# A spectral mixer with a token MLP, forward and backward, on one core: an opening put in another order, and more buffers for the last output

## Chip, cores, metric

The kernel runs on one core of one Trainium2 chip. The metric is device time in microseconds (us) of that core; lower is better. A profile is one execution with the hardware profiler on. Its span runs from the first to the last instruction and is about 2 us shorter than the time of the same run (367.6 us of 369.41 us for the kernel before).

## The reference

The reference is one layer with its gradients. `A_x` is 2048 tokens (S) by 448 features (D); F is 1792. All arrays are bfloat16.

```python
def _A_ref(x, w_r, w_i):                     # spectral mixer
    X = rfft2(x.astype(float32), axes=(-2, -1))
    X = X * (w_r + 1j * w_i)                 # (2048, 225)
    return irfft2(X, s=(S, D), axes=(-2, -1)).astype(bfloat16)

def _B_ref(x, w1, b1, w2, b2):               # MLP over the tokens
    h = layernorm(x)
    u = gelu(einsum("bsd,sf->bdf", h, w1) + b1)
    y = einsum("bdf,fs->bds", u, w2) + b2
    return y.transpose(0, 2, 1)

h   = x + _A_ref(layernorm(x), w_r, w_i)
out = h + _B_ref(layernorm(h), w1, b1, w2, b2)
# returned: out, then the gradients of x, w_r, w_i, w1, b1, w2, b2 for a given grad_out
```

## The kernel before

The Fourier transforms are matmuls. Their sine and cosine matrices are made on the core: GpSimd makes index patterns (iota), VectorE and GpSimd do the integer work, ScalarE takes the sine. The first transform goes tile by tile, 16 tiles of 128 tokens, each scaled by its LayerNorm factor (`rstd`).

In the gaps of the transform TensorE does "fill" work that doesn't depend on it: the matmuls of `w2` with `grad_out`, which the backward pass needs. For them `w2` must come in transposed, in 14 pieces of 128 x 2048 (512 KB each). A DMA transposes each piece on its way, into a ring of five buffers. All loads, transposes and stores are issued in program order by one engine, SyncE, so they form one queue. Its first part:

```python
    w2T_ring = Ring(ring(rE, 0, 3, NT, P).views + ring(rO, S, 2, NT, P).views)   # 5 buffers

    def load_w2T():
        j = w2T_ring.i
        if j == NFB:                         # NFB = 14
            return
        wT = w2T_ring.next()
        nc.sync.dma_start_transpose(out=wT, in_=B_w2[j * P:(j + 1) * P, :].rearrange("f (t c) -> f t c", c=P))
        w2Ts.append(wT)

    def load_x(q):                           # a quarter: 4 tiles of x, 448 KB
        nc.sync.dma_start(out=xn[:, 4 * q:4 * q + 4, :], in_=x_pt[:, 4 * q:4 * q + 4, :])

    load_x(0)
    load_go(0)                               # a quarter of grad_out
    load_w2T()
    load_go(1)
    load_x(1)
    load_go(2)
    load_go(3)
    load_w2T()
    load_x(2)
    load_w2T()
    load_x(3)
```

The fill lets the next transpose go when it is done with one; from the ninth on (`CAP = 8`) it holds them back until the second stage of the transform:

```python
    def dg_gen():
        for j in range(NFB):
            wT = w2Ts.pop(0)
            ...                              # 16 matmuls, one eviction
                    if w2T_ring.i >= cap[0]: # cap = [CAP]
                        held_w2.append(load_w2T)
                    else:
                        load_w2T()
...
    def fwd_x(c2):                           # at the start of the second stage
        if c2 == 0:
            for kind in "TWWWWTTT":          # T: a held transpose, W: a load of the imaginary weights w_i
                if kind == "W":
                    next(w_loads)
                elif held_w2:
                    held_w2.pop(0)()
```

The opening, and the point where the LayerNorm factors of tiles 4 and 5 come from GpSimd:

```python
    pcol = col()
    iota(pcol, [[0, 1]], 1)
    ...                                      # two more iotas
    r_ops = []
    gen_R(Later(ve, r_ops), Later(sc, r_ops))          # two 128x64 tensor_scalar first, then a Sin
    ...
    sc.activation(out=warm, in_=eps_x, func=ACT.Sqrt)  # fetches the square-root table
    zero_pads()                                        # four GpSimd memsets
    ...
    iota(base[:, :, :, 0], [[1, 16], [128, 16]])       # two 128x256 iotas
    ...
    for t in range(2):
        ln_stats(xn, t, mvx)
    ...
    Rs = {t: scale_R(t) for t in range(2)}
    for t in range(2, 4):
        ln_stats(xn, t, mvx)
    ...
    uv = gen_UV()                            # GpSimd: decode, masks
    ...
    for t in (4, 5):
        ln_stats(xn, t, mvx)
    newton_gp(mvx[:, 4:6, 1], rstd_x[:, 4:6], slice(4, 6))   # 1/sqrt on GpSimd
    fill(6)
```

The last work is the gradient of a weight, `gw_gen`. It evicts into a ring of six buffers (`ost`), and one store sends each buffer to memory:

```python
    ost = ring(rO, 0, 6, S // 2)

    def gw_gen(n, rhs, width, store):
        ...
                os_ = [ost.next(), ost.next()]
        ...
            def out(pw, w, c, i):
                evac(out=o[:, x:x + w], in_=pw[i][:, 0:w])
                if x:
                    defer(1.5, lambda j=2 * u + i: store(j, 512 * (c - 1), x + w, o), o)
```

Of the kernel before, what the change touches and what calls it, by code (L numbers as in the profile page):

```python
# [13 lines left out]
ALU = mybir.AluOpType  # L14
ACT = mybir.ActivationFunctionType
AX = mybir.AxisListType

P = 128
S = 2048
D = 448  # L20
# [99 lines left out]
def kernel(  # L120
# [20 lines left out]
    nc = tc.nc  # L141
# [4 lines left out]
    gp_ = nc.gpsimd  # L146
# [28 lines left out]
    def ps_mm():  # L175
        return psum.tile([P, 512], F32, tag="mm", bufs=4, name="ps_mm")
# [75 lines left out]
    def col(n=1):  # L252
        i = _ci[0]
        _ci[0] += n
        assert _ci[0] <= 64
        return cols[:, i:i + n]
# [32 lines left out]
    def load_w2T():  # L289
        j = w2T_ring.i  # L290
        if j == NFB:
# [4 lines that stand above are left out]
# [4 lines left out]
    def load_x(q):  # L300
        nc.sync.dma_start(out=xn[:, 4 * q:4 * q + 4, :], in_=x_pt[:, 4 * q:4 * q + 4, :])
# [1 line left out]
    def load_go(q):  # L303
        nc.sync.dma_start(out=go_tp[:, 4 * q:4 * q + 4, :], in_=go_tp_d[:, 4 * q:4 * q + 4, :])

    load_x(0)
    load_go(0)
    load_w2T()
    load_go(1)
    load_x(1)  # L310
    load_go(2)
# [13 lines left out]
    def ftmp(off, *dims):  # L325
        n = int(np.prod(dims))
        v = tf[:, off:off + n]
        if len(dims) == 1:
            return v
        names = "abcd"[:len(dims)]  # L330
        return v.rearrange("p (" + " ".join(names) + ") -> p " + " ".join(names),
                           **{c: d for c, d in zip(names, dims)})

    def iota(ap, pattern, ch=0):
        gp_.iota(ap, pattern=pattern, base=0, channel_multiplier=ch, allow_small_or_imprecise_dtypes=True)

    def floor_div(eng, out, in_, n):
        eng.tensor_scalar(out=out, in0=in_, scalar1=float(np.float32(1.0 / n)),
                          scalar2=float(-0.5 + 0.5 / n), op0=ALU.mult, op1=ALU.add)
        eng.tensor_scalar(out=out, in0=out, scalar1=MAGIC, scalar2=MAGIC, op0=ALU.add, op1=ALU.subtract)  # L340

    pcol = col()
    iota(pcol, [[0, 1]], 1)
# [49 lines left out]
    def gp_madd(out, in0, scalar, in1):  # L393
        gp_.tensor_scalar(out=gtmp, in0=in0, scalar1=scalar, scalar2=None, op0=ALU.mult)  # L394
        gp_.tensor_tensor(out=out, in0=gtmp, in1=in1, op=ALU.add)  # L395
# [33 lines left out]

    def decode(eng):  # L430
        a4, fc, s_, c_, f_ = col(), col(), col(), col(), col()
        floor_div(eng, a4, pcol, 64)
        gp_madd(s_, a4, -64.0, pcol)
        floor_div(eng, fc, s_, 8)
        gp_madd(s_, fc, -8.0, s_)
        gp_madd(s_, s_, 2.0, a4)
        floor_div(eng, c_, fc, 4)
        gp_madd(f_, c_, -4.0, fc)
        return fc, s_, c_, f_
# [77 lines left out]
    def gen_inv_cols(ch):  # L517
        e, en = col(), col()
        inv_cols[ch] = (e, en)
        gp_.memset(e, 2.0)  # L520
        if ch == 0:
            gp_.memset(e[0:1, :], 1.0)
        else:
            gp_.tensor_scalar(out=e, in0=pcol, scalar1=112.0, scalar2=None, op0=ALU.is_equal)
            gp_.tensor_scalar(out=e, in0=e, scalar1=-1.0, scalar2=2.0, op0=ALU.mult, op1=ALU.add)
            gp_.memset(e[0:1, :], 0.0)
        gp_.tensor_scalar(out=en, in0=e, scalar1=-1.0, scalar2=None, op0=ALU.mult)
        gp_.tensor_scalar(out=halves[:, ch:ch + 1], in0=e, scalar1=-0.5, scalar2=1.5, op0=ALU.mult, op1=ALU.add)
# [86 lines left out]

    def zero_pads():
        for f in fold_ring.views:
            gp_.memset(f[:, 896:912], 0.0)

    def fold_prep(src, t2):  # L620
        ft = fold_ring.next()
# [177 lines left out]
    def rstd_of(a, b):  # L799
        return newton(mvx[:, a:b, 1], rstd_x[:, a:b], slice(a, b))  # L800

    r_ops = []
    gen_R(Later(ve, r_ops), Later(sc, r_ops))
    warm = col()
    fwd_ops = gen_fwd_d()
    for fn in r_ops:
        fn()
    for fn in fwd_ops[:4]:
        fn()
    sc.activation(out=warm, in_=eps_x, func=ACT.Sqrt)  # L810
    zero_pads()
    base = ftmp(3072, 16, 16, 2)
    fix = ftmp(3584, 16)
    iota(base[:, :, :, 0], [[1, 16], [128, 16]])
    gp_.iota(base[:, :, :, 1], pattern=[[1, 16], [-128, 16]], base=1920, channel_multiplier=0,
             allow_small_or_imprecise_dtypes=True)
# [24 lines left out]
    fold_prep(xn, 1)  # L841
    for t in (4, 5):
        ln_stats(xn, t, mvx)
    newton_gp(mvx[:, 4:6, 1], rstd_x[:, 4:6], slice(4, 6))
    fill(6)
    turn_biases = load_biases()
    Meter.side, Meter.every, Meter.count = [], 1, 0
# [352 lines left out]
    ost = ring(rO, 0, 6, S // 2)  # L1200
    o4 = out_4.rearrange("(p t) f -> p t f", t=NT)

    def gw_gen(n, rhs, width, store):
        for u in range(n // 2):
            st = ahead.pop(0)

            def whole(pw, w, c, i, k, start, stop):
                mm(pw[i][:, 0:w], lhsT=st[:, 4 * i + k, :], rhs=rhs(c, k, 0, P), start=start, stop=stop)

            def parts(pw, w, c, start):  # L1210
                for i in range(2):
                    mm(pw[i][:, 0:w], lhsT=st[64 * i:64 * i + 64, 3, :], rhs=rhs(c, 3, 64 * i, 64 * i + 64),
                       start=start, stop=not start)

            def out(pw, w, c, i):
                o = os_[i]
                x = c % 2 * 512
                evac(out=o[:, x:x + w], in_=pw[i][:, 0:w])
                if x:
                    if c == 3 and i:  # L1220
                        st_load()
                    defer(1.5, lambda j=2 * u + i: store(j, 512 * (c - 1), x + w, o), o)

            for c in range(0, 4, 2):
                os_ = [ost.next(), ost.next()]
                pw = [ps_mm(), ps_mm()]
                for i in range(2):
                    for k in range(3):
                        whole(pw, 512, c, i, k, k == 0, False)
                        yield  # L1230
                w = min(512, width - 512 * (c + 1))
                pv = [ps_mm(), ps_mm()]
                parts(pw, 512, c, False)
                parts(pv, w, c + 1, True)
                for i in range(2):
                    out(pw, 512, c, i)
                yield
                yield
                for i in range(2):
                    for k in range(3):  # L1240
                        whole(pv, w, c + 1, i, k, False, k == 2)
                        if k == 2:
                            out(pv, w, c + 1, i)
                        yield

    pending.append(gw_gen(NFB, lambda c, k, a, b: goT[a:b, k, c * 512:(c + 1) * 512], S,
                          lambda j, a, n, o: nc.sync.dma_start(out=out_6[j * P:(j + 1) * P, a:a + n], in_=o[:, 0:n])))
    pending.append(gw_gen(NT, lambda c, k, a, b: du_t[a:b, 4 * c:min(NFB, 4 * c + 4), k, :], F,
                          lambda t, a, n, o: nc.sync.dma_start(out=o4[:, t, a:a + n], in_=o[:, 0:n])))
    nc.sync.dma_start(out=rC[:, 0:NG * 2 * KW], in_=w_d[:])  # L1250
    for t in range(NT - LAG, NT + 2):
        if t == NT - 2:
# [78 lines left out]
```

## Time and profile before

| | before |
|---|---|
| time, median of 3 runs | 370.2 us (369.69 to 370.56) |
| profiled span, mean granted clock | 367.6 us, 0.991 |
| TensorE busy | 346.1 us, 94% |
| TensorE idle, start of the span to the first matmul | 8.0 us |
| last matmul to the end of the span | 6.3 us |

In these lines PE is TensorE, PEld its weight loads, DVE VectorE, ACT ScalarE, POOL GpSimd, SP SyncE. The first fence is from the page of the kernel before: the span, each engine's busy time with its share and number of instructions, TensorE's busy tenths in 40 equal slices of the span, and the chain of waits by engine.

```profile
span 367.6 us, 6387 instructions
...
PE 346.1 (94%) x2114; PEld 185.8 (51%) x2121; DVE 255.8 (70%) x641; ACT 203.7 (55%) x426; POOL 73.7 (20%) x240
...
PE   1888999899999999999999999999999999999993
...
PE 77%; DVE 6%; POOL 5%; DMA 4%; ACT 4%; issue 2%; POOLq 0%; DVEq 0%; ACTq 0%
```

TensorE is nearly full except in the first and last slices, and it is most of the chain. The next fence is the table of stretches of the kernel before: from and to, length, then busy time (and instructions) of PE, PEld, DVE, ACT and POOL, the granted TensorE clock, the DMA engines' mean busy share (packets overlap, so it can pass 1), and GB/s.

```profile
0.00:14.00 14.00, 5.74 (x26) 2.95 (x27) 10.98 (x36) 7.32 (x14) 11.84 (x65) 1.00 0.92 253
14.00:30.00 16.00, 13.17 (x88) 7.82 (x86) 12.56 (x45) 8.67 (x18) 11.24 (x49) 0.89 1.14 220
30.00:46.00 16.00, 15.33 (x131) 10.89 (x132) 13.04 (x39) 12.49 (x25) 5.07 (x21) 1.00 1.06 199
46.00:62.00 16.00, 15.74 (x112) 9.62 (x110) 9.42 (x25) 9.20 (x20) 0.22 (x2) 1.00 1.03 194
```

TensorE leaves little time free after 30 us. (A share near 1 says that the engines are busy, not how many bytes they move: it goes with 194 to 253 GB/s here, and with 371 GB/s from 361 to 364 us.) From the timeline of the opening of the kernel before (start, duration, engine, line, operation, output and input; in brackets the idle time before it and what ended it):

```profile
1.25 0.49 POOL L335 IOTA r<- 128x448 f32 x1
1.32 2.08 DVE L79 TENSOR_SCALAR r<-r,cols 128x64 int32<-128x64 f32 x2
...
1.65 4.34 SPq L294 DMA_TRANSPOSE rE<-in_B_w_dram  x1
...
4.05 1.28 ACT L79 ACT_TABLE_LOAD   x1 [4.05 <-DVE r L79]
...
7.99 0.58 PE L215 MATMUL ps_ff<-rX,rS 128*128 128x128 bf16 x4 [7.99 <-DVE rX L79]
...
15.62 0.55 PE L215 MATMUL ps_mm<-rC,rE 128*128 128x448 bf16 x2 [0.54 <-DMA rE<-in_B_w_dram]
...
19.25 0.25 DVE L79 TENSOR_SCALAR rX<-Rm,rstd_x 128x128 bf16<-128x128 bf16 x1 [3.40 <-POOL rstd_x L376]
```

The 128x64 pair on VectorE takes 2.08 us, beside GpSimd's iotas. The sine table comes at 4.05 us, the first matmul at 7.99. At 15.62 TensorE waits for the second transpose of `w2`. At 19.25 VectorE has waited 3.40 us for GpSimd's `rstd`: that is the scaling of tile 4, which the rest of the opening follows.

From the same kernel, the queue of SyncE (how long the issue of each group held it) and TensorE around the tenth transpose:

```profile
41.54 5.96 SPq L655 DMA_DIRECT2D r<-r  x3
47.59 2.24 SPq L294 DMA_TRANSPOSE rO<-in_B_w_dram  x1
49.89 2.34 SPq L571 DMA_DIRECT2D rB<-in_A_w_i_dram  x4
52.34 4.30 SPq L294 DMA_TRANSPOSE rO<-in_B_w_dram  x1
...
59.52 0.55 PE L215 MATMUL ps_mm<-rC,rO 128*128 128x448 bf16 x2 [0.26 <-DMA rO<-in_B_w_dram]
```

`r<-r` are the reshapes of the first transform's result for the second stage. The tenth transpose is issued at 52.34 us and TensorE takes it up at 59.52. It waited only 0.26 us. And the end of the kernel before, where the last buffers wait for stores:

```profile
358.25 3.08 PE L215 MATMUL ps_mm<-r,rS 128*128 128x512 bf16 x18
...
360.83 0.86 ACT L79 CAST rO<-ps_mm 128x512 bf16<-128x512 f32 x2 [1.36 <-DMA out_dram<-rO]
362.17 1.02 DVE L79 CAST rO<-ps_mm 128x512 bf16<-128x512 f32 x2 [3.24 <-DMA out_dram<-rO]
...
363.82 0.81 SPq L1249 DMA_DIRECT2D out_dram<-rO  x2
```

### The profile page before, as it was taken

Reading aid. Unit: us, or ns where it says so; the run is one execution under the profiler, and the core shown is the slowest. Engines: PE = TensorE matmul, PEld = TensorE weight load, DVE = VectorE, ACT = ScalarE, POOL = GpSimd, SP = SyncE. Lnnn points to the kernel's source line nnn. Section 1 sums busy time; section 2 is a strip of 40 time slices with the busy share of each in tenths; the row PEclk is TensorE's granted clock in tenths of the full one; section 3 lists DMA queues with packets and bytes.
Section 4 is the critical chain, followed back from the end, with each engine's and each line's share of the span. In section 5 each row is a group of like instructions: output and inputs, shape, how many; then the busy total and the mean of one; then the engine's idle time right before and its main releaser. Section 6 shows DMA issues by size and latency. Waiting matters only on the chain.

```text
span 367.6 us, 6387 instructions
## 1 busy us (share of the span) xinstructions
PE 346.1 (94%) x2114; PEld 185.8 (51%) x2121; DVE 255.8 (70%) x641; ACT 203.7 (55%) x426; POOL 73.7 (20%) x240
## 2 busy tenths in 40 slices
PE   1888999899999999999999999999999999999993
PEld 0455766455645555555555566653444444555541
DVE  7698839973876888583247766674787883788881
ACT  3738748756966454413312454463576664576751
POOL 8867000000220000010002221100000000465650
PEclk9989999999999999999999999999999999999998
DMA  8999989648999999998868789379669899798997
GB/s 205 308 219 215 168 202 183 146 130 288 294 293 351 326 305 244 190 289 183 189 154 167 157 188 171 75 227 312 208 204 231 242 199 261 241 201 273 203 211 231
DMA packets 148249, 81.63 MB, mean 222 GB/s; under 512 B 95544, under 2 KB 140600, under 8 KB 147832
## 3 DMA queue, kind: packets, MB, share of 16 engines
q1 hardware_dynamic: 148216, 81.23, 90.3%
q8 instruction: 16, 0.26, 0.3%
q14 instruction: 17, 0.14, 0.1%
HBM read 27.56 MB, written 23.89 MB: 140 GB/s over the span
## 4 chain that ended last, share of the span: by engine, by line
PE 77%; DVE 6%; POOL 5%; DMA 4%; ACT 4%; issue 2%; POOLq 0%; DVEq 0%; ACTq 0%
PE ps_mm L215 62%; PE ps_ff L215 15%; DMA out_dram<-rO 2%; DMA rO<-in_B_w_dram 2%; DVE rS L79 2%; ACT rO L79 2%; DVE r L79 1%; ACT Ut L79 1%; DVE stats L79 1%; DVE rO L79 1%; DVE rA L79 1%; POOL cols L394 1%; POOL cols L395 1%; DVE rX L79 1%; ACT rAT L79 0%
## 5 line engine op out<-in xcount | busy, mean ns | idle before, releaser
L215 PEld LDWEIGHTS <-r 128*128 128x128 bf16 (+1 forms) x628 | 60.3, 105 | 49.2 <-issue 1.8
L215 PEld LDWEIGHTS <-rS 128*128 128x128 bf16 (+2 forms) x528 | 44.8, 99 | 48.6 <-issue 10.1
L79 ACT CAST rO<-ps_mm 128x512 bf16<-128x512 f32 (+1 forms) x75 | 40.3, 567 | 25.0 <-PE ps_mm L215 21.6
L1130 POOL TENSOR_SCALAR lcol<-lcol 128x1 f32<-128x1 f32 x32 | 18.6, 580 | 148.0 <-ACT r L79 148.0
L215 PE MATMUL ps_mm<-rD,r 128*128 128x448 bf16 x224 | 44.5, 352 | 0.0
L79 DVE CAST rO<-ps_mm 128x512 bf16<-128x512 f32 (+1 forms) x45 | 28.4, 644 | 19.3 <-PE ps_mm L215 16.0
L215 PEld LDWEIGHTS <-rst 128*128 128x128 bf16 (+1 forms) x320 | 24.0, 97 | 29.0 <-issue 13.1
L215 PE MATMUL ps_mm<-rC,rE 128*128 128x448 bf16 x144 | 37.1, 377 | 0.8 <-DMA rE<-in_B_w_dram 0.5
L79 ACT CAST r<-ps_ff 128x452 bf16<-128x452 f32 x54 | 28.9, 537 | 11.0 <-PE ps_ff L215 10.6
L215 PE MATMUL ps_mm<-rG,rst 128*128 128x512 bf16 (+1 forms) x155 | 34.0, 380 | 0.2
L215 PE MATMUL ps_mm<-rB,r 128*128 128x448 bf16 x160 | 31.1, 352 | 0.1
L215 PE MATMUL ps_mm<-r,rst 128*128 128x512 bf16 (+3 forms) x160 | 31.2, 353 | 0.0
L79 ACT ACTIVATE r<-ps_mm,rstd_h 128x448 bf16<-128x448 f32 x16 | 10.1, 634 | 29.3 <-PE ps_mm L215 29.3
L215 PE MATMUL ps_ff<-csI,rAT 113*128 113x448 bf16 x108 | 24.9, 353 | 0.4 <-ACT rAT L79 0.2
L79 DVE SCALAR_TENSOR_TENSOR r<-ps_mm,b2col,r 128x448 bf16<-128x448 f32 x16 | 10.9, 682 | 19.9 <-PE ps_mm L215 18.4
L79 ACT ACTIVATE r<-rC 128x448 bf16<-128x448 bf16 x16 | 9.1, 571 | 26.8 <-DMA out_dram<-r 21.8
L79 ACT ACTIVATE rG<-rG 128x896 bf16<-128x896 bf16 x14 | 13.3, 950 | 14.9 <-DVE rG L79 14.7
L215 PE MATMUL ps_mm<-rE,rS 128*128 128x448 bf16 x112 | 21.5, 352 | 0.0
L215 PEld LDWEIGHTS <-rO 128*128 128x128 bf16 (+1 forms) x165 | 15.6, 98 | 10.9 <-DMA rO<-in_B_w_dram 0.6
L79 ACT CAST rS<-ps_ff 128x512 bf16<-128x512 f32 x30 | 17.7, 589 | 5.1 <-PE ps_ff L215 5.1
L215 PEld LDWEIGHTS <-rE 128*128 128x128 bf16 x148 | 14.6, 103 | 9.6 <-issue 2.8
L215 PE MATMUL ps_mm<-rC,rO 128*128 128x448 bf16 x80 | 19.1, 352 | 0.3 <-DMA rO<-in_B_w_dram 0.3
(173 smaller groups left out, 604.3 us busy)
## 6 DMA issues: line engine op xcount, KB each, us to landing
out_dram<-rO SPq DMA_DIRECT2D x44, 256.0 KB
r<-in_B_w_dram SPq DMA_DIRECT2D x5, 1024.0 KB
r<-r SPq DMA_DIRECT2D x16, 226.0 KB
r<-r SPq DMA_DIRECT2D x32, 113.0 KB
rS<-in_B_w_dram SPq DMA_DIRECT2D x4, 896.0 KB
out_dram<-r SPq DMA_DIRECT2D x32, 112.0 KB
out_dram<-rO SPq DMA_DIRECT2D x16, 192.0 KB
rO<-in_B_w_dram SPq DMA_DIRECT2D x2, 1024.0 KB
```

Source lines behind the costliest of these rows:

```text
L79: fn(**kw)
L215: nc.tensor.matmul(out, lhsT=lhsT, rhs=rhs, start=start, stop=stop)
L394: gp_.tensor_scalar(out=gtmp, in0=in0, scalar1=scalar, scalar2=None, op0=ALU.mult)
L395: gp_.tensor_tensor(out=out, in0=gtmp, in1=in1, op=ALU.add)
L1130: gp_.tensor_scalar(out=m1, in0=ms, scalar1=-1.0 / D, scalar2=None, op0=ALU.mult)
```

## The change

The change wants TensorE to start earlier and to stop later work from waiting.

- ScalarE loads the sine table at once, by a dummy sine.
- Half a quarter of x comes first, then the first transpose, then grad_out and the other half.
- GpSimd's big iotas wait for a VectorE copy (`pcolb`) and a memset, so that they don't run beside VectorE's first operations; the pad memsets go to VectorE.
- Twelve idle matmuls on zeros are to raise TensorE's clock.
- The `rstd` of tiles 4 and 5 moves from GpSimd to VectorE.
- The last output gets 14 buffers in place of 6: eight in a region (`rG`) that is free by then.

```diff
-    load_x(0)
+    nc.sync.dma_start(out=xn[:, 0:2, :], in_=x_pt[:, 0:2, :])
+    load_w2T()
     load_go(0)
-    load_w2T()
+    nc.sync.dma_start(out=xn[:, 2:4, :], in_=x_pt[:, 2:4, :])
     load_go(1)
@@
+    warm = col()
+    nc.vector.memset(warm, 0.0)
+    sc.activation(out=warm, in_=warm, func=ACT.Sin)
+    nc.vector.memset(rAT[:, 0:512], 0.0)
+    idle = ps_mm()
+    for _ in range(12):
+        nc.tensor.matmul(idle[:, 0:D], lhsT=rAT[:, 0:P], rhs=rAT[:, 0:D], start=True, stop=True)
@@ decode, and one more place
-        floor_div(eng, a4, pcol, 64)
-        gp_madd(s_, a4, -64.0, pcol)
+        floor_div(eng, a4, pcolb, 64)
+        gp_madd(s_, a4, -64.0, pcolb)
@@ zero_pads, now called before gen_R
-            gp_.memset(f[:, 896:912], 0.0)
+            nc.vector.memset(f[:, 896:912], 0.0)
@@
+    pcolb = col()
+    ve.tensor_copy(out=pcolb, in_=pcol)
+    nc.vector.memset(base[:, 0, 0:1, 0], 0.0)
+    nc.vector.memset(base[:, 0, 0:1, 1], 0.0)
     iota(base[:, :, :, 0], [[1, 16], [128, 16]])
@@
-    newton_gp(mvx[:, 4:6, 1], rstd_x[:, 4:6], slice(4, 6))
+    for fn in rstd_of(4, 6):
+        fn()
@@
-    def gw_gen(n, rhs, width, store):
+    def gw_gen(n, rhs, width, store, ost):
@@ the first call passes ost, the second
+                          Ring(ring(rG, 0, 8, S // 2).views + ost.views)))
```

More of the change, by code (lines that the diff above doesn't have):

```diff
@@ L523, in gen_inv_cols @@
         else:
-            gp_.tensor_scalar(out=e, in0=pcol, scalar1=112.0, scalar2=None, op0=ALU.is_equal)
+            gp_.tensor_scalar(out=e, in0=pcolb, scalar1=112.0, scalar2=None, op0=ALU.is_equal)
             gp_.tensor_scalar(out=e, in0=e, scalar1=-1.0, scalar2=2.0, op0=ALU.mult, op1=ALU.add)
@@ L800, in rstd_of @@
         return newton(mvx[:, a:b, 1], rstd_x[:, a:b], slice(a, b))
+    zero_pads()
     r_ops = []
     gen_R(Later(ve, r_ops), Later(sc, r_ops))
-    warm = col()
     fwd_ops = gen_fwd_d()
@@ L810 @@
     sc.activation(out=warm, in_=eps_x, func=ACT.Sqrt)
-    zero_pads()
     base = ftmp(3072, 16, 16, 2)
     fix = ftmp(3584, 16)
+    pcolb = col()
+    ve.tensor_copy(out=pcolb, in_=pcol)
+    nc.vector.memset(base[:, 0, 0:1, 0], 0.0)
+    nc.vector.memset(base[:, 0, 0:1, 1], 0.0)
     iota(base[:, :, :, 0], [[1, 16], [128, 16]])
@@ L1246 @@
     pending.append(gw_gen(NFB, lambda c, k, a, b: goT[a:b, k, c * 512:(c + 1) * 512], S,
-                          lambda j, a, n, o: nc.sync.dma_start(out=out_6[j * P:(j + 1) * P, a:a + n], in_=o[:, 0:n])))
+                          lambda j, a, n, o: nc.sync.dma_start(out=out_6[j * P:(j + 1) * P, a:a + n], in_=o[:, 0:n]), ost))
     pending.append(gw_gen(NT, lambda c, k, a, b: du_t[a:b, 4 * c:min(NFB, 4 * c + 4), k, :], F,
-                          lambda t, a, n, o: nc.sync.dma_start(out=o4[:, t, a:a + n], in_=o[:, 0:n])))
+                          lambda t, a, n, o: nc.sync.dma_start(out=o4[:, t, a:a + n], in_=o[:, 0:n]),
+                          Ring(ring(rG, 0, 8, S // 2).views + ost.views)))
     nc.sync.dma_start(out=rC[:, 0:NG * 2 * KW], in_=w_d[:])
```

## The prediction

> **What bounds the kernel now.** TensorE: the page gives it 346.1 us busy of a 367.6 us span; the chain of waits is matmuls for 77%. Its idle time sits mostly at the ends (timeline, stretches): 8.0 us before the first matmul, 2.4 us between 14 and 20 us, 6.2 us after the last matmul ends at 361.3. Its clock is 0.5 from 20 to 23.7 us.
>
> **The opening before.** The chain up to 19.25 us is almost all GpSimd.
> 1. VectorE's two 128x64 tensor_scalar start at 1.32 us and last 2.08 us together, ending when GpSimd's run of iotas and memsets ends (3.31 us). The Trainium skill (SBUF — State Buffer, "SBUF: two separate sides") says that VectorE in a two-port mode and GpSimd lock each other out for a whole instruction. The times agree; the cause isn't shown.
> 2. ScalarE loads the sine table only at 4.05 us (1.28 us), the square-root table at 5.76; the first matmul starts at 7.99.
> 3. GpSimd decodes until 15.1 us, then computes the rstd of tiles 4 and 5 until 19.2; VectorE waits 3.40 us for it, TensorE 1.88 us behind. Then VectorE is full to 27 us, then ScalarE, then TensorE from 30.67.
>
> **What the change does.**
> - Sine table load at about 0.8 us and a quieter GpSimd: square-root table about 2 us earlier, first matmul on data at about 6.3 us.
> - The rstd of tiles 4 and 5 costs VectorE nine tiny operations, estimated 1.4 us (0.15 us is its 128x2 reciprocal), in place of the 3.40 us wait. With the earlier start it scales tile 4 at about 16.3 us, not 19.25.
> - GpSimd's decode starts about 1 us later, behind a VectorE copy, but leaves the chain.
> - Loads: half of x first, then the weight transpose, whose issue holds the sync queue (4.34 us before), so grad_out and the other half of x go up to 4 us later. TensorE already waited 0.54 us for the second transpose at 15.62 us; that lands about then again, so TensorE gains nothing before 16 us. The gain comes after: the 1.88 us stall, 1.01 us at 30 us, part of the half-clock 3.7 us.
> - Idle matmuls: 12, about 0.37 us each when cold (estimate from the cold ones at 8.4 us), done at about 6 us: they delay nothing, and what they warm is then limited by loads.
> - End: the last evictions wait for output DMAs (ScalarE 1.4, VectorE 3.24 us); VectorE's last ends at 363.2, some 1.3 us later than it could. With 14 buffers that goes; but DMA moves 347 to 383 GB/s from 361 to 364 us, so about 1 us is won.
>
> **Sum.** Opening 3.2 us, end 1.0 us, all on the path, as TensorE is the chain from 31 us on: 370.2 - 4.2 = **366.0 us**, range 363.3 to 368.6. Chances: faster by over 2% 0.08, within 2% 0.90, slower 0.02.
>
> **What would show it.** Sine table load in the first 1.5 us; the 128x64 pair well under 1 us; VectorE's wait for that rstd gone; first matmul on data near 6.3 us; TensorE still waiting for a weight transpose at 15 to 16.5 us; TensorE full from 27 us instead of 31; last matmul to the end 5 us instead of 6.2. TensorE's busy time rises by 4 to 5 us of idle matmuls, no loss.
>
> **What would make it wrong.** The second half of x or grad_out landing after 8 us would undo the early start. GpSimd's rstd of tiles 6 and 7, behind a later decode, could be the new wait. The weight loads (DMA is near full from 8 to 28 us) could hold TensorE until 20 us and take the opening's gain; if they keep up, the opening gives 5 us. If bytes alone set the finish, the end gives nothing.

## The result, and the profile after

The kernel after takes 370.15 us (median of 4 runs, 369.84 to 370.57), against 370.38 us before (4 runs, 369.69 to 370.91). Ratios in this document are the mean time of one kernel's fast runs over that of the other's of the same rounds, so not quite the ratio of the medians quoted. Here it is 0.9996 with a 95% interval of 0.9976 to 1.0016: the same time. The predicted 366.0 us (363.3 to 368.6) was wrong.

Lines of the page of the kernel after:

```profile
span 368.3 us, 6392 instructions
...
PE 349.4 (95%) x2133; PEld 186.9 (51%) x2133; DVE 256.7 (70%) x659; ACT 204.1 (55%) x427; POOL 72.3 (20%) x226
...
PE 80%; DMA 5%; DVE 5%; ACT 5%; issue 1%; SPq 1%; POOL 0%; ACTq 0%
```

GpSimd has left the chain, as wanted, and DMA has gained a share. TensorE's added busy time, 3.3 us, is less than its 4.52 us of idle matmuls, so its other work has not become longer. The opening in the timeline of the kernel after:

```profile
0.72 1.28 ACT L79 ACT_TABLE_LOAD   x1 [0.72 <-PEq L1329]
...
1.21 4.52 PE L349 MATMUL ps_mm<-rAT 128*128 128x448 bf16 x12 [1.21 <-DVE rAT L346]
...
1.33 0.56 DVE L79 TENSOR_SCALAR r<-r,cols 128x64 int32<-128x64 f32 x2
...
4.72 0.50 SPq L309 DMA_DIRECT2D rA<-in_A_x_dram  x1
...
6.44 0.38 PE L215 MATMUL ps_ff<-rX,rS 128*128 128x128 bf16 x4 [0.71 <-DVE rX L79]
...
8.73 1.15 DVE L79 BATCH_NORM_STATS2 stats<-rA 128x6 f32<-128x448 bf16 x2 [2.19 <-DMA rA<-in_A_x_dram]
...
17.02 0.55 PE L215 MATMUL ps_mm<-rC,rE 128*128 128x448 bf16 x2 [0.62 <-DMA rE<-in_B_w_dram]
...
18.33 0.22 DVE L79 TENSOR_SCALAR rX<-Rm,rstd_x 128x128 bf16<-128x128 bf16 x1
```

The parts work one by one. The sine table comes at 0.72 us. The 128x64 pair takes 0.56 us, not 2.08. The first matmul on data starts at 6.44 us, not 7.99. Not all of this need be the change's doing. One run of the experiments below (`end_only`) has the opening of the kernel before, iotas and all, and its timeline shows:

```profile
1.33 0.71 DVE L79 TENSOR_SCALAR r<-r,cols 128x64 int32<-128x64 f32 x2
...
6.92 0.59 PE L215 MATMUL ps_ff<-rX,rS 128*128 128x128 bf16 x4 [6.92 <-DVE rX L79]
```

The other six profiles with that opening have 2.08 us and 7.99 us. So the long pair comes in six of the seven profiles of the old opening, and in the seventh TensorE starts 1.07 us earlier too; by 37 us nothing is left of that (`end_only` is not ahead of the others there). In the kernel after, the 3.40 us wait for GpSimd is gone. But the second half of the first x quarter lands only at 8.73 us, and tile 4 is scaled at 18.33 us: 0.92 us earlier than before, where the prediction had 16.3.

The queue of SyncE and TensorE around the tenth transpose, kernel after:

```profile
40.58 5.96 SPq L664 DMA_DIRECT2D r<-r  x3
46.63 2.59 SPq L294 DMA_TRANSPOSE rO<-in_B_w_dram  x1
49.28 2.35 SPq L580 DMA_DIRECT2D rB<-in_A_w_i_dram  x4
51.73 5.00 SPq L294 DMA_TRANSPOSE rO<-in_B_w_dram  x1
...
60.37 0.55 PE L215 MATMUL ps_mm<-rC,rO 128*128 128x448 bf16 x2 [2.07 <-DMA rO<-in_B_w_dram]
```

The reshapes go out 0.96 us earlier than before. The tenth transpose goes out 0.61 us earlier, because the one ahead of it held the queue longer. Yet TensorE takes it up 0.85 us *later*, and its wait is 2.07 us, not 0.26. The stretches that show the gain and its loss, kernel after:

```profile
30.00:46.00 16.00, 16.00 (x136) 11.19 (x135) 12.40 (x36) 12.48 (x24) 3.95 (x19) 1.00 1.09 212
46.00:62.00 16.00, 13.93 (x101) 8.54 (x100) 10.08 (x25) 7.73 (x17) 0.11 (x1) 1.00 1.04 181
```

TensorE has 0.67 us more busy time from 30 to 46 us, and 1.81 us less from 46 to 62 us. The DMA engines are full in both. The end, kernel after:

```profile
358.28 3.73 PE L215 MATMUL ps_mm<-r,rS 128*128 128x512 bf16 x21
...
361.17 0.92 ACT L79 CAST rG<-ps_mm 128x512 bf16<-128x512 f32 x2 [1.03 <-PE ps_mm L215]
361.21 1.26 DVE L79 CAST rG<-ps_mm 128x512 bf16<-128x512 f32 x2 [1.60 <-PE ps_mm L215]
...
363.81 0.85 SPq L1262 DMA_DIRECT2D out_dram<-rG  x2
```

No eviction waits for a store now. VectorE's last ends at 362.47 us, 0.46 us after the last matmul, where before it ended 1.86 us after it. The last two stores are issued at 363.81 us all the same, and the span ends 6.3 us after the last matmul (368.3 less 362.01), as before (367.6 less 361.33, also 6.3).

**TensorE's lead.** To follow the gain through the run, I matched each matmul on data with the same matmul of the kernel before, in program order, and took the difference of their starts. Minus means earlier than in the profile of the kernel before. I call it the lead, and give it at the time that the kernel before has. For the kernel after it is -0.96 us at 37 us, -0.96 at 58, +0.85 at 62 and -0.05 at 106. So what the opening won is whole until 58 us, and is lost in one step at the tenth transpose; what was lost beyond that comes back in the second stage. Each lead is from one profile: kernels with the same opening as before differ by up to 0.5 us at 37 us and 1 us by 87 us, and I don't read less than that from a single lead. The profile of the kernel before is itself a late one: four of the kernels below that have the same opening (`end_only`, `before_short`, `before_short5`, `before_swap`) stand at -0.35 to -0.48 us at 37 us and at -0.69 to -0.89 at 106. Against these the kernel after has about 0.5 us at 37 us, not 0.96, and is behind at 106.

### The profile page after: what moved, and what is told of

The parts are those of the page before. It is cut to its first block, busy times and chain, and to the rows that moved or that the text cites. A ratio compares the mean times of both kernels' runs of the same rounds, so it can differ in the third digit from the quotient of the medians.

```text
span 368.3 us, 6392 instructions
## 1 busy us (share of the span) xinstructions
PE 349.4 (95%) x2133; PEld 186.9 (51%) x2133; DVE 256.7 (70%) x659; ACT 204.1 (55%) x427; POOL 72.3 (20%) x226
## 4 chain that ended last, share of the span: by engine, by line
PE 80%; DMA 5%; DVE 5%; ACT 5%; issue 1%; SPq 1%; POOL 0%; ACTq 0%
PE ps_mm L215 65%; PE ps_ff L215 15%; DMA rO<-in_B_w_dram 2%; DMA r<-rD 2%; ACT rO L79 2%; DVE stats L79 2%; ACT rG L79 1%; DMA rA<-in_A_x_dram 1%; DVE r L79 1%; ACT Ut L79 1%; SPq L294 1%; DVE rA L79 1%; DVE rS L79 0%; ACT rX L79 0%; DVE mvx L79 0%
## 5 line engine op out<-in xcount | busy, mean ns | idle before, releaser
L215 PE MATMUL ps_mm<-rC,rE 128*128 128x448 bf16 x144 | 36.3, 369 | 3.3 <-DMA rC<-in_grad_out_dram 2.7
L79 ACT CAST rO<-ps_mm 128x512 bf16<-128x512 f32 (+1 forms) x52 | 28.5, 582 | 14.9 <-PE ps_mm L215 12.7
L215 PE MATMUL ps_mm<-rG,rst 128*128 128x512 bf16 (+1 forms) x160 | 35.0, 380 | 0.0
L79 DVE CAST rO<-ps_mm 128x512 bf16<-128x512 f32 (+1 forms) x28 | 18.1, 658 | 11.8 <-PE ps_mm L215 11.8
L215 PE MATMUL ps_ff<-csF,rS 112*128 112x226 bf16 x128 | 17.7, 261 | 1.7 <-ACT rS L79 1.7
```

The costliest lines, as they stand in the source:

```text
L79: fn(**kw)
L215: nc.tensor.matmul(out, lhsT=lhsT, rhs=rhs, start=start, stop=stop)
```

## The experiments

**My theory (A in the expectations): the queue of loads.** Reshapes, transposes of `w2` and weight loads go through one queue, and the DMA engines are full to 62 us. The queue runs just behind TensorE. A lead of TensorE makes it wait for the next thing from the queue, and the lead is gone.

**Rivals.** (1) The new order of loads at the opening spoils the gain; with the old order it would stay. (2) VectorE and ScalarE, not the queue, set the pace of the second stage (E in the later expectations). (3) The idle matmuls cost more than they bring. (4) At the end, buffers were the limit and something else ate the gain. The expectations below: another letter in one of them is a rival of those runs only.

There were 18 runs, in five rounds of kernels on five chips, each with its own runs of the kernel before. Each kernel has 6 runs, beside 11 of the kernel before, and is correct where not said otherwise.

### First rounds: the parts

**Only the end**: the kernel before with the 14 buffers.

```diff
-    def gw_gen(n, rhs, width, store):
+    def gw_gen(n, rhs, width, store, ost):
@@ second call
+                          Ring(ring(rG, 0, 8, S // 2).views + ost.views)))
```

> The kernel before with only the 14 output buffers of the last weight gradient. Theory A (the bytes still to be stored set the finish): the last evictions end about 0.5 us after the last matmul instead of 1.85 us, the distance from the last matmul to the end of the span stays at 6.1 to 6.4 us, ratio 0.998 to 1.002. Rival B (my prediction: the wait for buffers was on the path): that distance falls to about 5.2 us, ratio 0.997. Rival C (the change's two parts cancel: the end's buffers cost what the opening wins, by a late transpose of du at 302 us): about 0.7 to 1 us slower, with a wait of about 1 us for that transpose.

Measured: 1.0015 (0.9990 to 1.0041), 369.12 us against 369.16. The buffers alone bring nothing that the times show. In the profile the end takes 5.9 us, between the 6.1 to 6.4 of theory A and the 5.2 of rival B.

**Only the opening**: the kernel after with the six old buffers.

```diff
-                          Ring(ring(rG, 0, 8, S // 2).views + ost.views)))
+                          ost))
```

> The changed kernel with the old six output buffers. Theory A (the opening's lead is taken back at 58 to 60 us by a weight transpose that does not come earlier): TensorE about 0.9 us ahead of before until 58 us, then a wait of 1.5 to 2.5 us for that transpose, no lead after 90 us, ratio 0.998 to 1.002. Rival C (the two parts cancel): 0.7 to 1 us faster, ratio about 0.9975.

Measured: 1.0026 (1.0000 to 1.0053), 370.11 us against 369.16. The lead is -0.70 us at 58 us and +0.91 at 62: the same step as in the kernel after. So neither part hides a gain that the other takes back.

**The old order of loads**: the kernel after with the kernel before's order at the opening (rival 1).

```diff
-    nc.sync.dma_start(out=xn[:, 0:2, :], in_=x_pt[:, 0:2, :])
-    load_w2T()
+    load_x(0)
     load_go(0)
-    nc.sync.dma_start(out=xn[:, 2:4, :], in_=x_pt[:, 2:4, :])
+    load_w2T()
```

> The changed kernel with the loads in the order of before (whole first load of x, grad_out, then the weight transpose). Theory A: tiles 2 and 3 are there when VectorE comes for them, the 2.19 us wait for x is gone, tile 4 is scaled at 15.5 to 17 us instead of 18.33, TensorE waits instead for the second weight transpose at about 15 us, and reaches 57 us 1.5 to 3 us ahead of before; the wait at 58 to 60 us grows by just that much (3 to 5 us), and the time is 0.997 to 1.002 of before. Rival D (the lead would be kept, only the second half of x was late): 2 to 3 us faster than before, ratio 0.992 to 0.995.

Measured: 1.0027 (1.0005 to 1.0049), 369.99 us against 369.16. From its timeline:

```profile
16.43 0.22 DVE L79 TENSOR_SCALAR rX<-Rm,rstd_x 128x128 bf16<-128x128 bf16 x1
...
17.12 0.55 PE L215 MATMUL ps_mm<-rC,rE 128*128 128x448 bf16 x2 [1.84 <-DMA rE<-in_B_w_dram]
...
60.20 0.55 PE L215 MATMUL ps_mm<-rC,rO 128*128 128x448 bf16 x2 [1.96 <-DMA rO<-in_B_w_dram]
```

The old order does give the opening more: tile 4 is scaled at 16.43 us, and the lead at 37 us is -1.84, not -0.96. But TensorE waits 0.66 us for the last reshape at 49.73 us and 1.96 us for the tenth transpose. The lead is -1.02 at 58 us, +0.68 at 60 and +2.10 at 62, and the time is no better. The last 1.4 us are not a wait: the clock record of this profile shows half clock from 61.22 to 64.63 us, after the waits. Rival 1 is right about the opening and wrong about the end time.

**More transposes before the second stage**: the kernel after with `CAP` at 10, so that the ninth and tenth transposes go early.

```diff
-CAP = 8
+CAP = 10
```

> The changed kernel with ten instead of eight weight transposes let go before the second stage, so that those that TensorE awaits at 58 to 60 us are issued near 35 us. Theory A: that wait of 2.07 us goes, the lead of 0.9 us is kept at 62 us, and what is kept of it after 90 us shows whether anything else takes it: 0.5 to 2 us faster if nothing does (ratio 0.995 to 0.9985). Rival E (the second stage is bound by VectorE and ScalarE, the wait for the transpose is only where it shows): wait gone but the same position at 87 us, ratio 0.999 to 1.001. If DMA has no room between 35 and 47 us, the reshape before 50 us comes late: a new wait there and a slower kernel.

Measured: 1.0122 (1.0088 to 1.0155), 373.73 us against 369.16. Now TensorE waits 3.5 us for the last reshape at 50 us (waits view: `r<-r`, one wait). The two transposes now go out at 36.47 and 44.02 us, and the last three reshapes at 48.44 us; in the kernel after those went out from 40.58. Moving a load forward in a full queue moves another one back.

### Taking bytes out of the queue

To test the theory itself, I took bytes away. This also shortens the time that a transpose holds SyncE: in the last of these kernels the tenth holds it for 1.19 us, where the kernel after has 5.00. So these runs test the queue as a whole, and don't tell bytes on the DMA engines from time on SyncE. In the next six kernels the late transposes load 2 of 16 blocks only, so some results (the MLP's weight gradients among them) are wrong; instructions on the other engines stay.

```diff
-        nc.sync.dma_start_transpose(out=wT, in_=B_w2[j * P:(j + 1) * P, :].rearrange("f (t c) -> f t c", c=P))
+        n = NT if j < 8 else 2
+        nc.sync.dma_start_transpose(out=wT[:, 0:n, :],
+                                    in_=B_w2[j * P:(j + 1) * P, 0:n * P].rearrange("f (t c) -> f t c", c=P))
```

**Six short transposes (j from 8), in the kernel before, the kernel after, and the kernel after with the old order of loads:**

> Wrong on purpose: the kernel before, with the last six of the fourteen weight transposes cut to an eighth of their bytes (the rest of the tile keeps an older tile's values). It is the base for the next two. Theory A: the small wait for a transpose at 59.5 us goes; the time at 87 us falls a little, since the reshapes of that stage have the queue to themselves: 0 to 2 us faster than before.

> Wrong on purpose: the changed kernel with the same six transposes cut. Theory A (their loads take the lead back): TensorE keeps its lead of about 0.9 us over before_short through 62 and 87 us, and is about 0.9 us faster than before_short, ratio to it 0.9975. Rival E (VectorE and ScalarE bound that stage): no wait for a transpose, but both kernels at the same place at 87 us, ratio to before_short 1.000.

> Wrong on purpose: the changed kernel with the old order of the first loads and the same six transposes cut. Its lead at 31 to 50 us was 1.84 us with the full loads. Theory A: that lead is kept past 87 us: about 1.8 us faster than before_short (ratio 0.995), less up to 0.8 us if the reshape at 50 us stays late. Rival E: same as before_short.

Measured, all against the same runs of the kernel before:

| | ratio (95%) | median us (before: 368.45) | lead at 37 us | lead at 62 us |
|---|---|---|---|---|
| before, short | 1.0021 (0.9987 to 1.0056) | 368.72 | -0.47 | -0.91 |
| after, short | 0.9974 (0.9951 to 0.9998) | 367.87 | -1.16 | -0.57 |
| old order, short | 0.9977 (0.9957 to 0.9997) | 367.90 | -2.04 | -0.64 |

The step at the tenth transpose is gone. But the lead still doesn't stay: in the two kernels with the new opening TensorE now waits for the last reshape at 50 us, 0.9 and 1.7 us. I had looked at one transfer; the whole queue ahead of it is the limit. The theory was widened: any transfer of the queue from 50 us on can take the lead.

**Nine short transposes (j from 5), so that the reshapes come sooner too:**

```diff
-        n = NT if j < 8 else 2
+        n = NT if j < 5 else 2
```

> Wrong on purpose: the kernel before with the last nine of the fourteen weight transposes cut to an eighth, so that three fewer full ones run between 24 and 34 us, ahead of the reshape that TensorE needs at 50 us. The base for the next two. Theory A: little or no change of its time against before (0 to 2 us faster), since its engines, not its loads, were last before 50 us.

> Wrong on purpose: the changed kernel with the same nine transposes cut. Theory A, widened (the queue of loads as a whole is the wall: first the reshape at 50 us, then the transpose at 60 us): no wait for a DMA between 40 and 62 us, and the lead over before_short5 of 0.5 to 1 us at 37 us is still there at 62 us. What is left at 87 us tells whether VectorE and ScalarE bound the second stage (rival E: nothing left).

> Wrong on purpose: the changed kernel with the old order of the first loads and the same nine transposes cut. Theory A, widened: the lead over before_short5 at 37 us is 1.4 to 2.4 us and is kept to 62 us, and 0.997 to 0.994 of before_short5 in time if nothing else binds. Rival E: the lead is lost between 62 and 87 us with waits for VectorE or ScalarE, not DMA.

| | ratio (95%) | median us (before: 369.0) | lead at 37 us | lead at 62 us | lead at 106 us |
|---|---|---|---|---|---|
| before, short | 0.9990 (0.9962 to 1.0017) | 368.39 | -0.47 | -0.91 | -0.82 |
| after, short | 0.9974 (0.9937 to 1.0011) | 367.15 | -1.25 | -1.68 | -1.40 |
| old order, short | 0.9938 (0.9917 to 0.9958) | 366.67 | -1.74 | -2.18 | -1.63 |

TensorE has no wait at all between 40 and 62 us in the two kernels with the new opening. Their lead over "before, short" is the same at 62 us as at 37: 0.77 and 0.78 us in the one, 1.27 and 1.27 us in the other. **The same cut in bytes is worth 0.1% with the opening of before, and about 0.9% with the new opening and the old order of loads** (1.0027 with all bytes, 0.9938 without; those two are of different rounds). The intervals of the first and the third row don't overlap. One caveat: the third kernel has 14 output buffers and the first has six; in the first one's profile TensorE waited 1.1 us for evictions of outputs (0.8 us at 318 us and 0.3 at 349). The second row's interval overlaps the first's, so of the kernel after itself only the profile, not the times, shows it.

By 106 us 0.2 to 0.45 us of those leads are lost, less than the spread between profiles. So nothing here gives rival 2 more than a small part.

### Is it the other engines (rival 2)? Are the idle matmuls a cost (rival 3)?

**Less fill in the second stage**: with fewer fill matmuls between the steps of the second stage, TensorE needs each transpose later, but VectorE and ScalarE get less time per step.

```diff
-    s2_stage(fwd_x, fwd_mult, ML_F, 3, 24, True)
+    s2_stage(fwd_x, fwd_mult, ML_F, 2, 24, True)
```

> The changed kernel with two instead of three fill matmuls per step of the second stage, so that TensorE needs the ninth and tenth transposed weight later and the rest of the fill work runs after the stage. Theory A: the 2.07 us wait at 58 to 60 us goes or falls under 0.5 us, the stage's reshapes are hidden behind the fills left over, and the kernel is 0.5 to 2 us faster than before (ratio 0.995 to 0.9985). Rival E: waits for VectorE and ScalarE grow by what the wait for the transpose loses; ratio 0.999 to 1.003.

Measured: 1.0091 (1.0066 to 1.0115), 372.23 us against 369.0. The wait for the tenth transpose is gone, and TensorE waits for VectorE instead, 4.3 us in six waits (`DVE rS` in the waits view). So rival 2 names a limit that lies close by, but not the one at which TensorE waits around 60 us in the kernel after.

**One idle matmul, not twelve:**

```diff
-    for _ in range(12):
+    for _ in range(1):
```

> The changed kernel with one idle matmul instead of twelve. If the idle matmuls' warm clock is worth nothing since TensorE then waits for loads and its clock falls back at 8.9 us: same place at 20 us within 0.3 us, same time, ratio to before 0.998 to 1.003. If the warm clock helps, or the idle matmuls delay the first data matmul, it moves at 20 us by over 0.5 us.

Measured: 0.9995 (0.9958 to 1.0031), 370.35 us against 370.17. In this profile the lead is -0.02 us at 20 us, -0.24 at 37 and +0.87 at 62: it ends at the same place. Rival 3 isn't seen: idle matmuls cost nothing that is measurable. They may even bring something at the opening. The kernel after has -0.64 us at 20 us, so the move of 0.62 us is over the 0.5 us that the expectation set as the mark of a warm clock that helps, and the eight profiles with the new order of loads and twelve idle matmuls have -0.70 to -1.44 at 37 us. It is one profile, and the time shows nothing of it, as what is won there is lost by 62 us.

### One part of the opening alone

**The kernel before with the `rstd` of tiles 4 and 5 on VectorE**, and nothing else.

```diff
-    newton_gp(mvx[:, 4:6, 1], rstd_x[:, 4:6], slice(4, 6))
+    for fn in rstd_of(4, 6):
+        fn()
```

> The kernel before with one part of the change: the rstd of tiles 4 and 5 on VectorE (1.77 us there, measured) instead of behind GpSimd's decode. If that part alone makes the opening's lead, TensorE is 1 to 1.8 us ahead of before at 37 us, as much as or more than the whole change's 0.96 us, and the sine load, the held iotas and the new load order add nothing to it. If the sine load and the load order carry the lead, it is under 0.6 us. Either way Theory A expects the lead to be gone by 62 us and a ratio of 0.998 to 1.002.

Measured: 1.0002 (0.9962 to 1.0042), 370.88 us against 370.17. From its timeline:

```profile
17.58 0.22 DVE L79 TENSOR_SCALAR rX<-Rm,rstd_x 128x128 bf16<-128x128 bf16 x1
...
50.25 0.35 PE L215 MATMUL ps_ff<-r,Vt 128*128 128x452 bf16 x1 [1.05 <-DMA r<-r]
```

This one edit gives a lead of -1.70 us at 37 us, **more than the whole change (-0.96)**. And it ends no sooner: 1.05 us go at the last reshape, about as much at the tenth transpose (1.06 us of wait). The lead is +0.31 us at 62 us. The new opening isn't needed to see the loss.

### Can the queue be arranged to keep the lead?

If it is the order in the queue that binds, then sending another transpose ahead of the four loads of imaginary weights should get TensorE its tenth transpose in time, unless those loads then come too late.

```diff
-            for kind in "TWWWWTTT":
+            for kind in "TTWWWWTT":
```

**In the kernel after:**

> The changed kernel with the tenth weight transpose issued ahead of the four loads of the imaginary weights instead of after them. If one late transfer is the wall at 60 us, its wait of 2.07 us goes, nothing new comes, and it is 1 to 2 us faster (ratio 0.995 to 0.998). Theory A, widened (the queue as a whole is the wall): the wait moves to the imaginary weights, seen as waits of ScalarE or VectorE for them and of TensorE for those engines; ratio 0.999 to 1.004.

Measured: 0.9960 (0.9920 to 1.0001), 369.37 us against 370.17. The best correct kernel by its ratio, but its interval reaches 1. The lead is kept past the transpose (-1.45 at 62 us, -1.52 at 106). Against the profiles of the old opening, at -0.69 to -0.89 by then, that is 0.6 to 0.8 us. ScalarE now waits 1.77 us for the imaginary weights, and TensorE 1.69 us for ScalarE at 67 us (0.89 in the kernel before). Later, at 302 us, this profile has a wait of 2.12 us for another DMA (`r<-rD`, the transposed `du` of the backward pass). The kernel after has 1.0 us there, most others none. It comes and goes between profiles with the same code there, so I tie it to no part of the change.

**The kernel before with the VectorE `rstd`, the swap and the 14 buffers; the kernel after with the old order of loads and the swap; the kernel before with the swap alone:**

> The kernel before with three small edits: the rstd of tiles 4 and 5 on VectorE, the tenth weight transpose ahead of the imaginary weights' loads, and the 14 output buffers. If the experiments are read rightly: a lead of 1.7 us at 37 us, about 0.5 us of it left after the reshape at 50 us, no wait for a transpose at 60 us, 1 to 2 us ahead of before at 106 us, and 0.5 to 2 us faster in time (ratio 0.9945 to 0.9985), which would beat both kernels. If the queue of loads is a wall however it is ordered: ahead by under 0.5 us at 106 us and a ratio of 0.999 to 1.002.

> The changed kernel with the old order of the first loads and the same swap in the second stage. The same reading: a lead of 1.8 us at 37 us, a wait of about 0.7 us for the reshape at 50 us, none for a transpose at 60 us, 1 to 2 us ahead at 106 us, ratio 0.9945 to 0.9985. If its sine load, held iotas and idle matmuls are worth nothing, it ends where newton_swap_rings does, within 0.5 us.

> The kernel before with only the swap in the second stage. It has no lead to keep and waited only 0.26 us for the transpose: ahead by 0 to 0.7 us at 106 us, ratio 0.998 to 1.002. If the swap alone gives the 0.996 of the changed kernel with the swap, the opening has no part in that gain.

| | ratio (95%) | median us (before: 368.68) | lead at 37 us | lead at 62 us | lead at 106 us |
|---|---|---|---|---|---|
| before, rstd, swap, buffers | 1.0001 (0.9973 to 1.0028) | 368.68 | -1.71 | -1.89 | +0.10 |
| after, old order, swap | 0.9984 (0.9960 to 1.0008) | 368.56 | -1.27 | -1.51 | +0.33 |
| before, swap | 1.0023 (0.9995 to 1.0050) | 369.64 | -0.48 | -0.91 | -0.89 |

The swap moves the loss to 67 us and doesn't end it. From the timeline of the first of the three:

```profile
59.48 0.95 ACT L79 COPY rG<-rB 64x900 bf16<-64x900 bf16 x1 [2.45 <-DMA rB<-in_A_w_i_dram]
...
67.32 0.35 PE L215 MATMUL ps_ff<-r,Vt 128*128 128x452 bf16 x1 [2.37 <-ACT rX L79]
```

ScalarE waits for the imaginary weights until 59.48 us and TensorE then waits for ScalarE. **In the four kernels with the swap that copy starts at 59.24, 59.48, 59.53 and 59.67 us, while their leads at 37 us go from -0.48 to -1.71.** TensorE goes on at 67.08 to 67.51 us in all four, and at 67.44 in the kernel before. A time that doesn't move when everything ahead of it does is the mark of another limit.

Something else takes part after it: in the first two kernels of the table the clock record shows half clock for 3.41 us right then (from 67.71 and from 69.20 us), and 1.4 and 1.3 us of lead go without a wait. The other two have none, which goes with their better leads at 106 us. The six runs of the first kernel fall apart in the same way: three with a mean granted clock of 0.991 to 0.992 took 369.5 to 370.2 us, three with 0.995 to 0.997 took 367.4 to 367.8. Only one of them has a profile, so I can't say that it is this stretch in all three.

With the old order in the queue it is the tenth transpose that stays. In the eight profiles that keep that order, all bytes, the fill and `CAP`, TensorE waits for it every time and takes it up between 59.4 and 60.6 us.

### The end

**The last stores sent earlier (rival 4)**: in the kernel after, the other outputs of the last stage, the gradients of the spectral weights, are worked out and stored sooner, so that fewer bytes are left for the end.

```diff
-    GW_AT = (4, 9, 11, 11, 12, 13, 14, 15)
+    GW_AT = (2, 4, 5, 6, 7, 8, 9, 10)
```

> The changed kernel with the eight stores of the spectral weight gradients issued at tiles 2 and 4 to 10 of the last stage instead of 4 and 9 to 15, so that none is left for the end. Theory A (bytes set the finish): the distance from the last matmul to the end of the span falls from 6.3 us to 5 us or less and the kernel is 0.5 to 1.5 us faster than the changed one (ratio to before 0.9965 to 1.000). Rival B (only the buffers matter): the distance stays at 6 us or more.

Measured: 1.0161 (1.0130 to 1.0192), 374.67 us against 368.45. From the last matmul to the end it now takes 3.6 us (369.26 to 372.9) where the kernel after takes 6.3, with about 0.5 MB moved in it and not 1.5. But the kernel loses about 7 us ahead of it: between 340 and 353 us TensorE waits for VectorE and ScalarE (`DVE rG` 3.2 us, `ACT rG` 1.8 us in the waits view), as these weight gradients are work for them, put where they have no room, and the clock record then shows half clock from 353.82 to 357.23 us. And one pair of small-row stores held SyncE's queue for 4.50 us. As a kernel it is a miss. As a test it isn't clean either: fewer bytes went with a shorter end, but TensorE ended 7 us later, and stores could go on in that time. Buffers do little: with 14 of them in the kernel before the same stretch takes 5.9 us, with six in the kernel after 6.0. Over the other correct kernels it is 5.7 to 6.3 us with 14 and 6.3 to 6.6 with six, so they may bring some 0.4 us (an estimate from the means of these profiles), which no time shows.

## Why the prediction was wrong

Of the 4.2 us that it promised, about 2.2 were never won at the opening, about 1.0 were won and lost again by 62 us (both by the one profile of the kernel before, which is a late one), and the 1.0 at the end didn't come.

**Right.** The sine table at 0.72 us. The Trainium skill (ScalarE: Activation LUTs, "What ACT_TABLE_LOAD costs") gives about 1283 ns for such a load; here it is 1.28 us in both kernels, and the change moves it, it doesn't remove it. The 128x64 pair well under 1 us (0.56; but 0.71 in one profile of the old opening). The wait for GpSimd's `rstd` gone. First matmul on data near 6.3 us (6.44). TensorE still waiting for the second transpose, though at 17.02 us rather than 15 to 16.5. Idle matmuls of 0.37 us each (4.52 us for twelve), no loss. Of what it said would show, three sizes were off with the gain itself: TensorE full from 29.71 us, not 27; 6.3 us from the last matmul to the end, not 5; 3.3 us more busy time, not 4 to 5. Loads limit what the idle matmuls warm: the Trainium skill (TensorE: Matmul & The Clock Gate, "Part 1: The HAM clock gate") says that the clock halves after an idle window of about 3.4 us. In the clock record of the kernel after it was up at about 5.5 us and at half again from 8.9 to 15.7. The steps there are multiples of 3.413 us, which agrees. The idleness doesn't: from 5.5 to 8.9 us TensorE was busy for 1.35 us, and its longest wait was 1.34 us, for grad_out.

**Wrong: "Opening 3.2 us".** The mechanism was right and the size off. VectorE's work from the statistics of tiles 2 and 3 to tile 4 is one unbroken list, so the sum can be checked: 19.25 us before, less the 3.40 us wait, plus 0.72 us because those statistics start at 8.73 us and not at 8.01, plus 1.77 us for the nine tiny operations (one each 0.2 us, 15.36 to 17.13) gives 18.34; the timeline has 18.33. The prediction counted on a start about 1 us *earlier* and on 1.4 us for the nine. The start is the bigger error, 1.7 us: the second half of x stood behind the transpose in the queue and landed late. The prediction named this danger ("the second half of x or grad_out landing after 8 us would undo the early start") and still counted the gain. With the old order those statistics start at 6.81 us, and tile 4 is scaled at 16.43: the predicted 16.3 was the figure for another order of loads. Even then only 1.84 us of lead came out at 37 us; on the way there VectorE waits 0.91 us for the third quarter of x (at 18.17), and TensorE 1.84 us for the second transpose.

**The step that failed: "all on the path, as TensorE is the chain from 31 us on".** TensorE was the chain, but not with room behind it. The queue of loads ran 0.26 us behind it at 59.52 us. That small wait meant that the transpose came *just* late, so that everything TensorE gained before it would turn into waiting. The runs showed this from three sides. Leads at 37 us of 0.70, 0.96, 1.70 and 1.84 us (opening only, after, `rstd` alone, old order) are all gone after the tenth transpose (part of the last two at the reshape before it), which TensorE takes up at 60.43, 60.37, 59.83 and 60.20 us, later than the 59.52 of before. Without the bytes, 0.77 and 1.27 us of lead pass 62 us untouched. With the order changed, a loss appears at the next load in the queue. None of the edits that only sped up the opening made the kernel faster.

**Wrong: "so about 1 us is won" at the end.** The waits of the evictions did go. They weren't on the path: the last stores were issued at 363.82 us before and 363.81 after. The buffers did fill a gap: from 364 to 366 us the DMA engines' share was 0.57 and 0.76 in the kernel before, 1.06 and 1.03 in the kernel after. But in both some 1.5 MB were still to be moved when the last matmul ended (237 and 245 GB/s over 6.3 us), and in the kernel after that took 6.3 us again, with the engines full to 366 us. The prediction named this too ("if bytes alone set the finish, the end gives nothing"). The profiles fit it, with up to 0.4 us left for the buffers; no run settles it.

**What stays open.** With the changed opening the second transpose is taken up at 16.9 to 17.7 us in every profile, under either order of loads, against 15.4 to 15.9 us with the opening of before. Likewise the tenth comes somewhat later (60.2 to 60.6, against 59.4 to 59.8). No run takes the remaining parts of the opening (sine table, iotas, pads, idle matmuls) apart one by one, so I can't say which does it. One idle matmul in place of twelve left the tenth at 60.39. Nor do the runs tell which part of the queue binds, the 16 DMA engines or the time that each issue holds SyncE: in the kernels before and after both are busy from 41.5 to 64.5 us almost without a gap, the short transposes relieved both, and no run issued some of the loads from another engine. And whether VectorE's 2.08 us for the 128x64 pair was really GpSimd in its way, as the Trainium skill (SBUF — State Buffer, "SBUF: two separate sides") would have it. The pair ended with GpSimd's run in the kernel before, which fits; but it took 0.71 us beside the same iotas in `end_only`, and the 0.56 us of the kernel after lie beside the 128x448 iota, which was not moved. No run changed the iotas alone.

No correct kernel beats both the kernel before and the kernel after beyond doubt.

## What to carry to other kernels

Before counting a gain as kept, look for the next limit downstream: a small wait for a DMA on a full queue (here 0.26 us) doesn't mean that the DMA is nearly harmless, but that it has no slack, and what an engine gains ahead of it can be waited away there. Test it by taking bytes out of the queue, with wrong results if need be: if a lead then survives, it is the queue that has to be made shorter, not the engines faster. And look at the clock record after each long wait: half clock can cost as much as the wait did (1.3 to 1.4 us after waits of 2.0 to 2.4 us here).

## What the Trainium skill lacked or had wrong

- **DMA: Bandwidth & Descriptors, "Issuing engines are not separate DMA queues"**, says that the time on the sequencer to start a DMA is usually small relative to the DMA itself. For the transposes here it isn't: the tenth held SyncE's queue for 4.30 us of the 7.13 us from issue to landing before (5.00 of 8.59 us after), and the second for 5.24 and 6.39 us. How much of that is waiting for room behind earlier transfers the profile doesn't show.
- **Advanced Engine Details and Errata, "X-Bar Transpose (TRN2)"**, says that transposes are as fast as regular DMAs. No run here compares their bandwidth. It says nothing of the time of issue, and that differs: in the kernels before and after a 512 KB transpose held the queue for 1.9 to 6.4 us in the first 36 us, a 448 KB plain load of x for 0.40 to 0.58 us.
- **Perfetto Trace Analysis** advises to work on what blocks TensorE where it idles. It has no word on the limit right behind the chain: here four kernels had lost leads of 0.7 to 1.84 us once past a transfer for which TensorE had waited just 0.26 us before.
- **TensorE: Matmul & The Clock Gate, "Part 1: The HAM clock gate"**, puts half clock after a window in which TensorE is idle. Here it came after windows in which TensorE was partly busy: in the 3.41 us before each of five such stretches it was busy for 1.0 to 1.5 us (before 20.02 us in the kernel before, 8.87 in the kernel after, 61.22 in `old_loads`, 67.71 in `newton_swap_rings`, 69.20 in `old_loads_swap`). Worked out from the 20 profiles, cut into windows of 3.413 us in step with the clock record, up to the last matmul: of the 19 windows at full clock with TensorE busy for 1.53 us or less, 18 were followed by half clock; of those busy for longer, none. This was read after the fact, and no run was made to test it.
